# A hand-ordered kernel of two mixers: a new order of all its steps, and more partial sums left to TensorE

## The chip, the cores and the metric

One core of one Trainium2 chip runs one program. Its five engines (TensorE, VectorE, ScalarE, GpSimd and SyncE, in the profile PE, DVE, ACT, POOL and SP) each work through a list of instructions in a fixed order and wait for one another by semaphores. The metric is the device time of one execution in microseconds, lower being better.

## The reference

Two mixers run on the same input of 2048 positions and 512 channels, and a gate of each position blends them. All tensors are bfloat16.

```python
def reference(A_u, A_A_re, ..., B_x, B_wqkv, B_w_phi, B_wo, gate_w):
    ...
        K = jnp.einsum("dn,dnl,dn->dl", Cc, P, dB).real      # P = exp(dt * A * l): a kernel of 2048 taps per channel
        ...
        Yf = Uf * Kf[None, :, :, :]                          # long convolution by a Fourier transform over 4096 points
        ...
        phi_q = jnp.concatenate([_softmax(pq, axis=-1), _softmax(-pq, axis=-1)], axis=-1)
        phi_k = jnp.concatenate([_softmax(pk, axis=-1), _softmax(-pk, axis=-1)], axis=-1)
        kv = jnp.einsum("bhsf,bhsd->bhfd", phi_k, v)         # 32 heads of 16
        z  = jnp.einsum("bhsf->bhf", phi_k)
        num = jnp.einsum("bhqf,bhfd->bhqd", phi_q, kv)
        den = jnp.einsum("bhqf,bhf->bhq", phi_q, z)[..., None] + 1e-6
    ...
    x = A_u
    g = _sigmoid((x * gate_w).sum(-1, keepdims=True))
    a = _A_ref(x, ...)                                       # the state space model, as a convolution, plus u * Dskip
    b = _B_ref(x, B_wqkv, B_w_phi, B_wo)                     # the linear attention
    return g * a + (1 - g) * b
```

## The kernel before

The program is a list of some 870 **steps**. A step is a Python function that issues a handful of instructions on one engine; `Plan.add` records its name, its engine, the steps it needs, and the buffers it takes from and gives back to small rings (`take`, `drop`). Nothing schedules them by rule: `Plan.run` issues them in the order of one string, `ORDER`, in which two digits of base 64 are the number of a step. What an engine does next, and in which sequence its queue issues transfers, is therefore the order of its own steps in that string. Steps that may run on either of two engines (the copies out of PSUM, as `XK` or `oT`, on ACT or DVE) take their engine from the string `SIDES`; steps that may take a PSUM buffer from either of two rings take it from `RINGS`.

The work, in the order in which it begins:

- *Tables and input.* Sines and exponentials for the Fourier matrices (`W1`, `TB`, `TI`, `TJ`) and for the state space model (`Ctab`, `Dtab`, `Gtab`). The input `UD` is turned by TensorE (`xps`) and copied to `xT` (eight steps, each on DVE or ACT). `udc` copies `UD` into the layout `UDp` that the Fourier stages want (eight steps of a quarter of a half, DVE or ACT). `sel1` multiplies two small masks into `selE` (DVE or POOL).
- *Keys and input spectrum.* For 8 pairs of position blocks: `pk` (TensorE), its exponentials `ek` (ACT), the sums of 16 features `zk`, `vp`, `vb`, `vr`, and `kn`, which adds to `kvp`. A pair with a 1 in the string `ZPS` first lets TensorE add four by four (`zp`, 8 matmuls), so that DVE reduces one 128x512 tile to 128x128 (L739); a pair with a 0 has DVE reduce two 128x1024 tiles (L736). Between them `psAu`, `psBu` transform the input, and the result goes to memory (`xuw`). `kvbd` builds the block matrices of the attention from `kvp` after the last `kn`.
- *Units and queries.* The 512 channels are 16 **units** of 32. Unit U has DVE multiply the tables `Ctab` and `Dtab` twice (`A1`, `A2`, L1101), which makes two halves of the tile `A`. A unit with a 0 in the string `FOURS` then has DVE add the halves (`A3`, L1112) and TensorE multiply them with `R` (step `kps`, line 183) in 64 matmuls of 64 columns. A unit with a 1 leaves the addition out, and `kps` is 128 matmuls that add in PSUM. `R` comes from `cs` (two sines on ACT) and `E` (an exponential on ACT) by way of `El`, `Rh`, `Rl` on DVE. ACT needs another function table for sines than for exponentials, so the sines are done in four groups of four units, with a table load (L65) on either side. Behind `kps` stand `KD` (copy out), `psA`, `XA`, then per quarter of the channels `psB`, `XK`, the product `t` with the input's spectrum (DVE; its input `XUX` is loaded by `xup`), `psz`, `Zr`, a store `zw` and a load `zr` that turn the tile by way of memory into `ZT`, `psy`, and the gated result `ou` (DVE). Steps of the last unit work on half tiles. The queries (`pq`, `eq`, `zs`, `z1` to `z5`, a store `aw` and a load `ar` that spread the normalisers into `ax`, `em`, `ops`, `oT`) lie between them; the fourth query block is `pqL` and so on, and `bpsL` with `bsg` makes its output. `ax` and `ZT` share a single buffer, so each load of it waits for the last reader before it.
- *Output.* `out` and `outL` store from `xT`; each of the steps `out` may be issued from SP or from ACT.

```python
    def run(self):
        ...
        for n in self.nodes:
            n.at = n.eng if isinstance(n.eng, str) else n.eng[int(next(sides, 0))]
        ...
        for i in order:
            n = self.nodes[i]
            ...
            n.fn()
```

A 4-term unit is made by this line of `kgen_chunk`:

```python
            terms = [(k, k) for k in range(2)] if not four else [(0, 0), (2, 0), (1, 1), (3, 1)]
```

Of the kernel before, what the change touches and what calls it, by code (L numbers as in the profile page):

```python
# [70 lines left out]
class Plan:  # L71

    DIGITS = "0123456789abcdefghijklmnopqrstuvwxyzABCDEFGHIJKLMNOPQRSTUVWXYZ-_"
    ORDER = ("040B0H0K0d0y0C0D0L0s0I070J0M0P0g000S110j0N08010z0T0m0Q0e2R0a0p0q0r0_0W2T100U0O0V14120Y2U2x0A2S050k130Z2y2V2X2Z0R190v0t0u"
             "0b0c0w2_0l0E0X2W1516172L1a061b2Y022-30311y33340n030f0-"
             "0h1e1f0i1w2J18321c0F0o2B2K2M1n1z1H1g1A1o2D2C1d1p1I091x1E1J351Q1R2F1B0x1C2E0G2H1q36372G2I2P382N2Q391F3b2O3c4C1S3a4J4L4K4M"
             "3d3e4Q4R3f4U1Y3g4N1r4O1h4V3h1L4Y4-"
             "4P3i4Z4_3j4W4S53542z57504T3k4X1Z515b5d58521s1D593l5c3n5i5e55565j3m5a1G3o5q5f5g5s5r5t3p3r3q1T5m5n5u3s5v5h5o5k5w5x5B1P4D4E"
             "3w2v5l5p4F5y5F5C3y1U5H3x5G5I5J5z5A1V5D5E3t3z5U3D5K5V5M5N3A3R3E2w3F5W5L1O5_3G5O5Q5X5Y5Z3B3C1W605R5S1N3K3M1K3S1M5-"
             "5P3L634G642A615T653N673T6869626a666m6n6o3U6p3V3W3X3Y6b6c6q6d6r6s1t3Z3H3-1X3_3O1i1j41401_4221431-"  # L80
             "1k1l204445466e272923222b282d4748243P491m2a4a2c2e4b4g2f4c2g4d252h2o4e4h4i4n1u4j3u3v2j4p2i2l2k2m2q2p6i262s4q4o1v4k2n4u2r2t"
             "6f4v4w6j4r3I2u4x4y4z6g4l8l3J4A8p8m6t6u6k6v8q3Q4f4s6x6h8k8o6l8n8r8s6y6z6w6A6C4m4t4B8C6G8t6I6K8w8x8y8u6B6H6J4H8D8v6L6M6N7d"
             "8z8A8E4I8B7e7f8I7g8F6F9e8Q8G8H9b6O6P8R7h7j7i6Q6R8J9f7M7N8S6S6T6U6Vaeaf7O8W8X8K7k9g8L8T8U8Z8-"
             "938M8N7l6D8_7m8V7n6W6X6Y8O8P8Y7P94an7o7pao7q6_70717r90917Qa47S9295ag7R6Z7s6-"
             "72aha8a9966Ea7akaca5ai73aa75979998ajap7677a69aalatamab74ad7TaBaC7t797u7v7U78au7y7z7V7w7x9caq9naras7AavaH7W9d9h9o9paw7X9v"
             "aY9waK7Y7ZaDaL9q9raZ7a9x9y9zaIc57B7-aM9kc69D9EaQaEbX9L7Cb_aF7D9M7_9Ac07EaRaG9iaxaz80ay9B818285bYaA7Ga-"
             "7IaJ86879j9Fc19s7Jb-"
             "9l9m9Na_7bc7aNaOaPc3cbb2b37HbZc283aS9C7FaT849G9H9I9t89aUaWaV8baX7cccc8c99O9u9P9Q9R888cb87Kb9b0c4caceb19J8abacfcgbg8dck9K"
             "8ecl8f8gbbbh8hbcbibob4cP9Sbpbqcd9T8ichci7L8jcBcCcjcsdYcYctcucycDczdZd-cQcR9Ucmd_cHcvcw9W9Xcnbj9VbwbkblbxcocIbre0eLcp9Ze1"
             "e2b5b6eMbse3eUeVcxb7bye4cqbtbu9Ybdbe9-"  # L90
             "9_cAcrcSbme5cZdOdScEbfcFcGcTcUe6a0a1bve7dTdRdWeNa2e8cJcKe9bzbAedeecLeRcNcOa3eSeaebeOcMc_ePbBd0ecd1d7cVd8d9cWeCdfcXeWdPdU"
             "d2daefege-e_eQd3dbdQdgeTdVd4dndodXdhdcg1g2dieDeEdjeXbKfAbCbnbDbEbFeYfBeZf0f1bGc-dpbLddg7dqbHd5f2drbMf3f4f5bNfGbIbJbOezdk"
             "eAfDdsfEeBeIf6f7feffdldtbPdebQdBfCfHehdueifFejdmf8fgeJd6ekdvfIfJdyf9fafhfbg4fifKg5g6dwfjdzfkfcdxdCdEfLdAdFfMg3g8dGg9dHfN"
             "fleFelfdfmfpdDdLgagbgcgddIeGemeKfqeHfOfPfQfRgeenepfneofreqeresgfggghgifSfTfUfofsbRgjbSgkdJftetglfVfYfZgmgngobUbVgqfufWdM"
             "dNbWgpf-fvfxfygreufwevewexbTeydKfzfXf_g0gvgwgsgtgugx")
# [564 lines left out]
def attention_keys(P, nc, g, psum, r):  # L660
# [40 lines left out]
    for s2 in range(8):  # L701
# [20 lines left out]

        def ps4(K=K, box=box, on=P.ZPS[s2] == "1"):
            if not on:
                return
            box.ps = bank("zk")
            for u in range(2):
                e = K.E[:, u].rearrange("p g (h a b) -> p (g h) a b", a=4, b=4)
                for k in range(4):
                    nc.tensor.matmul(box.ps[:, 256 * u:256 * u + 256], lhsT=g.ident[:], rhs=e[:, :, k, :], start=(k == 0), stop=(k == 3), skip_group_check=True)  # L730

        def rd(K=K, box=box, on=P.ZPS[s2] == "1"):
            K.Z = g.kwk.tile([128, 2, 2, 32], F32, name="Zk")
            if not on:
                for u in range(2):
                    nc.vector.tensor_reduce(out=K.Z[:, u].rearrange("p g h -> p (g h)"), in_=K.E[:, u].rearrange("p g (h f) -> p (g h) f", f=16),  # L736
                                            axis=mybir.AxisListType.X, op=ALU.add)
                return
            nc.vector.tensor_reduce(out=K.Z[:].rearrange("p u g h -> p (u g h)"), in_=box.ps[:].rearrange("p (z b) -> p z b", b=4), axis=mybir.AxisListType.X, op=ALU.add)  # L739
# [888 lines left out]
```

## Time and profile before

| | us |
|---|---|
| three runs | 265.06, 265.24, 267.37 |
| median | 265.24 |
| profiled execution, first to last instruction (span) | 263.7 |
| median above that span | 1.5 |
| DVE, ACT, PE busy within the span | 233.9, 221.3, 198.5 |
| mean granted TensorE clock | 0.916 of full speed |

The profile is of one execution. Its span leaves out what lies before the first and after the last instruction, and no time of its own is listed for it beside the span; the three runs lie 1.4 to 3.7 us above it, the median 1.5 us. "Busy" is the time in which an engine has at least one instruction under way. Two DVE or ACT instructions behind one another overlap a little, so the second of two adds less than its own duration.

### The profile page before, as it was taken

Reading aid. Unit: us, or ns where it says so; the run is one execution under the profiler, and the core shown is the slowest. Engines: PE = TensorE matmul, PEld = TensorE weight load, DVE = VectorE, ACT = ScalarE, POOL = GpSimd, SP = SyncE. Lnnn points to the kernel's source line nnn. Section 1 sums busy time; section 2 is a strip of 40 time slices with the busy share of each in tenths; the row PEclk is TensorE's granted clock in tenths of the full one; section 3 lists DMA queues with packets and bytes.
Section 4 is the critical chain, followed back from the end, with each engine's and each line's share of the span. In section 5 each row is a group of like instructions: output and inputs, shape, how many; then the busy total and the mean of one; then the engine's idle time right before and its main releaser. Section 6 shows DMA issues by size and latency. Waiting matters only on the chain.

```text
span 263.7 us, 10050 instructions
## 1 busy us (share of the span) xinstructions
PE 198.5 (75%) x4491; PEld 133.8 (51%) x4512; DVE 233.9 (89%) x315; ACT 221.3 (84%) x305; POOL 8.3 (3%) x21
## 2 busy tenths in 40 slices
PE   0755999999845688988565867889996678979770
PEld 0654656646634423446354245665674456764550
DVE  6799989888799989999999999999999999986630
ACT  6989999998899989998999899999998996744200
POOL 4700000000000000000000000000000000000000
PEclk9999999999995659997999579999999999998975
DMA  6899000454500885203343366239753599989576
GB/s 196 144 204 233 6 4 2 121 146 138 151 10 2 239 239 165 83 13 87 88 162 82 122 209 210 73 116 199 150 193 120 189 239 242 179 206 141 133 112 102
DMA packets 67547, 35.93 MB, mean 136 GB/s; under 512 B 46000, under 2 KB 62000, under 8 KB 67504
## 3 DMA queue, kind: packets, MB, share of 16 engines
q1 hardware_dynamic: 65648, 34.76, 55.0%
q10 hardware_dynamic: 1856, 0.52, 1.1%
q8 instruction: 35, 0.57, 1.0%
q14 instruction: 8, 0.07, 0.1%
HBM read 22.17 MB, written 13.11 MB: 134 GB/s over the span
## 4 chain that ended last, share of the span: by engine, by line
PE 32%; DVE 26%; ACT 13%; DMA 12%; issue 7%; SPq 7%; DVEq 0%; ACTq 0%
PE pk L709 5%; DMA ax<-apd 5%; PE vp L757 5%; DVE A L1101 3%; SPq L1494 3%; DMA ZT<-Zd 3%; DMA apd<-apm 3%; ACT cs L68 3%; DVE R L1123 2%; DVE R L1119 2%; PE psz L1265 2%; PE psA L591 2%; PE bps L946 2%; PE psB L616 2%; PE kvp L774 2%
## 5 line engine op out<-in xcount | busy, mean ns | idle before, releaser
L1101 DVE TENSOR_TENSOR A<-Ctab,Dtab 128x2048 bf16<-128x2048 bf16 x32 | 37.9, 1220 | 0.0
L68 ACT ACTIVATE cs<-args 128x1024 bf16<-128x1024 f32 x32 | 30.8, 1042 | 1.5 <-PE args L1023 1.5
L1265 PE MATMUL psz<-t,TI 128*128 128x512 bf16 x51 | 16.5, 414 | 6.2 <-DVE t L1233 4.6
L1123 DVE TENSOR_TENSOR R<-E,cs 128x2048 bf16<-128x2048 bf16 x16 | 19.5, 1219 | 0.1
L1119 DVE TENSOR_TENSOR R<-E,cs 128x2048 bf16<-128x2048 bf16 x16 | 19.5, 1219 | 0.0
L68 ACT ACTIVATE Ek<-pk 128x512 bf16<-128x512 f32 x32 | 16.7, 600 | 1.9 <-PE pk L709 1.6
L183 PE MATMUL kps<-R,A 128*32 128x64 bf16 x1536 | 17.2, 203 | 1.5 <-DVE A L1112 0.4
L183 PEld LDWEIGHTS <-A 128*32 128x32 bf16 x1536 | 15.3, 117 | 5.6 <-issue 2.0
L149 ACT CAST Zr<-psz 128x1024 bf16<-128x1024 f32 x15 | 15.5, 1032 | 3.2 <-PE psz L1265 1.5
L149 ACT CAST XA<-psA 128x1024 bf16<-128x1024 f32 (+1 forms) x15 | 14.7, 1017 | 3.4 <-PE psA L190 3.4
L757 PE MATMUL vp<-WW,xT 128*128 128x512 bf16 x59 | 16.9, 419 | 0.5 <-issue 0.3
L616 PE MATMUL psB<-XAu,TB 64*128 64x128 bf16 x256 | 11.8, 250 | 6.6 <-ACT xst L149 3.5
L1233 DVE TENSOR_TENSOR t<-XUX,XK 128x2048 bf16<-128x2048 bf16 x14 | 16.7, 1219 | 0.0
L68 ACT ACTIVATE E<-args 128x1024 bf16<-128x1024 f32 x16 | 16.4, 1036 | 0.3 <-PE args L1045 0.2
L68 ACT ACTIVATE Eq<-pq 128x512 bf16<-128x512 f32 (+1 forms) x28 | 16.5, 694 | 0.1
L149 ACT CAST XK<-psB 128x1024 bf16<-128x1024 f32 (+1 forms) x14 | 13.7, 993 | 2.8 <-PE psB L196 1.5
L843 PE MATMUL pq<-xT,Wqp 128*128 128x512 bf16 x64 | 15.4, 379 | 0.8 <-ACT xT L149 0.6
L709 PE MATMUL pk<-WW,xT 128*128 128x512 bf16 x58 | 15.0, 380 | 0.4 <-issue 0.2
L190 PE MATMUL psA<-W,KD 128*64 128x128 bf16 x256 | 10.7, 233 | 5.5 <-ACT KD L149 2.7
L616 PEld LDWEIGHTS <-TB 64*128 64x128 bf16 x256 | 9.7, 111 | 9.9 <-issue 9.8
L196 PE MATMUL psB<-XA,TB 128*128 128x128 bf16 (+2 forms) x192 | 10.6, 206 | 3.6 <-DVE XA L151 1.6
L190 PEld LDWEIGHTS <-KD 128*64 128x64 bf16 x256 | 8.5, 117 | 9.1 <-issue 5.2
(210 smaller groups left out, 502.0 us busy)
## 6 DMA issues: line engine op xcount, KB each, us to landing
XUX<-XUd SPq DMA_DIRECT2D x32, 256.0 KB
XUd<-xst SPq DMA_DIRECT2D x8, 512.0 KB
ax<-apd SPq DMA_DIRECT2D x16, 256.0 KB
Zd<-Zr SPq DMA_DIRECT2D x15, 256.0 KB
ZT<-Zd SPq DMA_DIRECT2D x6, 512.0 KB
UD<-in_A_u_dram SPq DMA_DIRECT2D x16, 128.0 KB
XUd<-xst SPq DMA_DIRECT2D x8, 256.0 KB
wqk<-in_B_wqkv_dram SPq DMA_DIRECT2D x1, 1024.0 KB
```

Of the source, the lines that this page charges most:

```text
L68: return self.nc.scalar.activation(**kw)
L149: self.nc.scalar.copy(out=o, in_=i)
L183: nc.tensor.matmul(kps[32 * dj:32 * dj + 32, g4, e, :], lhsT=A[:, d // 4, 32 * ka:32 * ka + 32, d % 4], rhs=R[:, kr, d, :], start=(i == 0) ...
L190: nc.tensor.matmul(ps[64 * ri:64 * ri + 64], lhsT=lhsT, rhs=fc.W1[:, ri].rearrange("p r d -> p (r d)"), start=True, stop=True, tile_positi ...
L616: nc.tensor.matmul(box.ps[:, c2, sl, :], lhsT=fc.TB[rows, b0:b0 + 2].rearrange("p a b -> p (a b)"), rhs=X.t[rows, k, r0 + sl].rearrange("p ...
L709: nc.tensor.matmul(box.ps[:], lhsT=xT[:, st, kt, :], rhs=g.WW[:, kt, :], start=(kt == 0), stop=(kt == 3))
L757: nc.tensor.matmul(box.ps[:], lhsT=xT[:, st, kt, :], rhs=g.WW[:, 4 + kt, :], start=(kt == 0), stop=(kt == 3))
L1101: nc.vector.tensor_tensor(out=c.A[:, :, 64 * k:64 * k + 64, :].rearrange("p q (x b) l -> p x b q l", b=8), in0=cf.unsqueeze(2).to_broadcas ...
L1119: nc.vector.tensor_tensor(out=c.R[:, :, :, 32:64], in0=t.E[:, 1].unsqueeze(1).to_broadcast([128, 2, 32, 32]), in1=t.cs[:], op=ALU.mult)
L1123: nc.vector.tensor_tensor(out=c.R[:, :, :, 0:32], in0=t.E[:, 0].unsqueeze(1).to_broadcast([128, 2, 32, 32]), in1=t.cs[:, ::-1, :, ::-1], o ...
L1233: nc.vector.tensor_tensor(out=box.t, in0=Ls[r0 // ns].X[:], in1=box.XK[:].unsqueeze(1).to_broadcast([128, 2, 1024]), op=ALU.mult)
L1265: nc.tensor.matmul(box.ps[:, hb, :], lhsT=fc.TI[:, k].rearrange("p t h a -> p (t h a)"), rhs=box.t[:, k, 512 * hb:512 * hb + 512], start=( ...
```

## The change

All of it is in the strings at the head of `Plan`. `ORDER` is another permutation of the same steps, made with steps that are dense in TensorE work put apart. `SIDES` and `RINGS` are other choices. `FOURS` has ones for units 0 to 14 (before: 1, 2, 3, 4, 7, 9, 11 and 12), so that units 0, 5, 6, 8, 10, 13 and 14 lose their `A3` on DVE and get 64 more matmuls each. `ZPS` has ones for the pairs 5, 6 and 7 (before also 1), so that pair 1 loses its 8 matmuls `zp` and gets two reductions in place of one. The other change of engine counts, by steps: `oT` three more on DVE and three fewer on ACT; `udc` three more on DVE; `xT` one more on DVE; `XK` two fewer on DVE; `sel1` from DVE to POOL; one `bs3` to ACT and one `bsg` to DVE; among the `out` steps, one from ACT to SP and one from SP to ACT.

```diff
 class Plan:
     ...
-    ORDER = ("040B0H0K0d0y0C0D0L0s0I070J0M0P0g000S110j0N08010z0T0m0Q0e2R0a0p0q0r0_0W2T100U0O0V14120Y2U2x0A2S050k130Z2y2V2X2Z0R190v0t0u"
...
+    ORDER = ("1d0405060B0C0D0d0e0f0y0z0A0s0t0u0H0I0J0M0L000708090g0h0i0j0k0l0P0Q0K0102030S0U0V0N2R2T0_2x0O0T0W0Y0m0n0o0a0b0c0X10111415"
...
-    FOURS = ("0111100101011000")
-    ZPS = ("01000111")
+    FOURS = ("1111111111111110")
+    ZPS = ("00000111")
```

What this does to the engines' lists shows at three places. Line numbers of the changed kernel are 4 smaller from line 100 on.

The first place is VectorE's list ahead of the keys, where the last `xT` tiles and the `udc` copies stand. Before:

```order
L383 TENSOR_TENSOR ppy<-psri,ppx 128x512
L151 COPY xT<-xps 128x1024 x2
L151 COPY UDp<-UD 128x2x8x64
L383 TENSOR_TENSOR ppx<-psri,ppx 128x512
L151 COPY xT<-xps 128x1024
L151 CAST XAu<-psA 128x256x4 x2
```

With the change:

```order
L379 TENSOR_TENSOR ppy<-psri,ppx 128x512
L147 COPY UDp<-UD 128x2x8x64
L379 TENSOR_TENSOR ppx<-psri,ppx 128x512
L147 COPY xT<-xps 128x1024
L147 COPY UDp<-UD 128x2x8x64 x2
L147 COPY xT<-xps 128x1024
L147 COPY UDp<-UD 128x2x8x64
L147 COPY xT<-xps 128x1024
L147 CAST XAu<-psA 128x256x4 x3
```

Three copies to `UDp` have come over from ScalarE and stand ahead of VectorE's last `xT`, of which it now has five in all.

The second place is VectorE's list for the units 14 and 15, up to the last instruction that the last `kps` needs. The row `A<-A` is the addition `A3`, `A<-Ctab` is `A1` or `A2`, `E<-E` is `El`, `R<-E` is `Rh` (the smaller line number) or `Rl`. Before:

```order
L1119 TENSOR_TENSOR R<-E,cs 128x64x32
L1101 TENSOR_TENSOR A<-Ctab_75,Dtab 128x64x8x4 x2
L1365 TENSOR_TENSOR xT<-psy,gT 128x4x128
L1053 TENSOR_TENSOR E<-E,Gtab 128x1024
L1123 TENSOR_TENSOR R<-E,cs 128x64x32
L1112 TENSOR_TENSOR A<-A 128x8x256
L1233 TENSOR_TENSOR t<-XUX,XK 128x2048 x2
L1101 TENSOR_TENSOR A<-Ctab_75,Dtab 128x64x8x4 x2
L1112 TENSOR_TENSOR A<-A 128x8x256
L1053 TENSOR_TENSOR E<-E,Gtab 128x1024
L1123 TENSOR_TENSOR R<-E,cs 128x64x32
```

With the change:

```order
L1115 TENSOR_TENSOR R<-E,cs 128x64x32
L1049 TENSOR_TENSOR E<-E,Gtab 128x1024
L1119 TENSOR_TENSOR R<-E,cs 128x64x32
L1361 TENSOR_TENSOR xT<-psy,gT 128x4x128
L1115 TENSOR_TENSOR R<-E,cs 128x64x32
L1097 TENSOR_TENSOR A<-Ctab_75,Dtab 128x64x8x4
L1229 TENSOR_TENSOR t<-XUX,XK 128x2048 x2
L1097 TENSOR_TENSOR A<-Ctab_75,Dtab 128x64x8x4
L1049 TENSOR_TENSOR E<-E,Gtab 128x1024
L1119 TENSOR_TENSOR R<-E,cs 128x64x32
L1097 TENSOR_TENSOR A<-Ctab_75,Dtab 128x64x8x4
L1108 TENSOR_TENSOR A<-A 128x8x256
```

The addition of unit 14 is gone, that of unit 15 stands last, and `Rh` of unit 15 has moved behind `Rl` of unit 14.

The third place is the end of SyncE's list: the stores `Zd<-Zr` (`zw`), the loads `ZT<-Zd` (`zr`), the stores of the result from L1382 (`out`) and L995 (`outL`). Before:

```order
L1188 DMA XUX<-XUd 128x1024 x2
L1287 DMA ZT<-Zd_0_122 64x32x64 x2
L1382 DMA out_dram<-xT 32x12x128 x4
L1278 DMA Zd_64_123<-Zr 128x1024
L1382 DMA out_dram<-xT 32x12x256 x2
L995 DMA out_dram<-xT 32x4x384 x2
L1287 DMA ZT<-Zd_64_123 64x32x32 x2
L1382 DMA out_dram<-xT 512x1x64 x4
L995 DMA out_dram<-xT 32x4x384 x2
L1382 DMA out_dram<-xT 512x1x64 x2
```

With the change:

```order
L1184 DMA XUX<-XUd 128x1024 x2
L1378 DMA out_dram<-xT 32x12x256 x2
L1283 DMA ZT<-Zd_0_122 64x32x64 x2
L1378 DMA out_dram<-xT 32x12x128 x2
L1274 DMA Zd_64_123<-Zr 128x1024
L1378 DMA out_dram<-xT 32x12x128 x2
L1378 DMA out_dram<-xT 32x12x256 x2
L1283 DMA ZT<-Zd_64_123 64x32x32 x2
L1378 DMA out_dram<-xT 512x1x64 x2
L991 DMA out_dram<-xT 32x4x384 x4
L1378 DMA out_dram<-xT 512x1x64 x2
```

Behind the last `ZT` load two of the four stores of 512 short rows are gone (ScalarE issues them now, ahead of its last copy out of PSUM), and two stores of long rows have come in their place; both stores of 256 columns now stand ahead of that load.

More of the change, by code (lines that the diff above doesn't have):

```diff
@@ L73 @@
     DIGITS = "0123456789abcdefghijklmnopqrstuvwxyzABCDEFGHIJKLMNOPQRSTUVWXYZ-_"
-    ORDER = ("040B0H0K0d0y0C0D0L0s0I070J0M0P0g000S110j0N08010z0T0m0Q0e2R0a0p0q0r0_0W2T100U0O0V14120Y2U2x0A2S050k130Z2y2V2X2Z0R190v0t0u"
[L75 to L95, printed above, removed]
@@ L100 @@
+    SIDES = ("111110011110111001000000111010001001001100001011100000000000010100001101111101000010100111000000000000000000000000000000"
+             "00000001000000010000000110010000000001000000010001001")
+    RINGS = ("101000001110111011100000000000000000000000100000000000000010111111100000001011100011010110001101000101101100111010011101"
+             "01000")
     WARM = ("000000000000000000000000000000000000000000000000000000000000000000000000000000000000000000000000000000000000000000000000"
```

21 lines of the change are left out of this document (17 added, 4 removed).

## The prediction

> **What bounds the kernel now.** I read the page's first part, then cut the span into six stages by what the engines wait for in the chain that ended last, and asked for the busy time of each engine in each.
>
> ```profile
> PE 198.5 (75%) x4491; PEld 133.8 (51%) x4512; DVE 233.9 (89%) x315; ACT 221.3 (84%) x305; POOL 8.3 (3%) x21
> ...
> 0.00:28.00 28.00, 13.89 (x160) 12.32 (x161) 23.54 (x56) 24.90 (x32) 8.33 (x21) 1.00 0.94 184
> 28.00:71.00 43.00, 42.42 (x749) 26.22 (x757) 37.60 (x52) 39.02 (x75) 0.00 (x0) 1.00 0.30 84
> 71.00:104.50 33.50, 22.15 (x312) 12.90 (x313) 32.34 (x55) 31.50 (x36) 0.00 (x0) 0.75 0.46 132
> 104.50:214.20 109.70, 84.28 (x2219) 55.44 (x2225) 107.81 (x117) 104.93 (x138) 0.00 (x0) 0.94 0.48 134
> 214.20:235.60 21.40, 18.77 (x472) 15.03 (x473) 20.86 (x20) 15.66 (x17) 0.00 (x0) 1.00 1.08 211
> 235.60:263.70 28.10, 17.03 (x585) 11.91 (x585) 11.79 (x17) 5.34 (x10) 0.00 (x0) 0.76 0.73 124
> ```
>
> The columns behind the length are busy time of PE, weight loads, DVE, ACT and POOL, then the granted TensorE clock. The 89% of DVE hide three regimes. From 28 to 71 us (keys and input spectrum) PE is busy 42.42 of 43.00 us: that stage is TensorE's. From 71 to 235.6 us DVE works 161.0 of 164.6 us, but up to 214.2 us ACT is hardly behind it (104.93 of 109.70): two engines share that bound. After 235.6 us both are mostly idle, and a chain of single steps sets the end. So DVE work is worth its time only in the middle, and only as far as ACT can follow.
>
> **The change part by part.** The prices:
>
> ```profile
> L1112 DVE TENSOR_TENSOR A<-A 128x2048 bf16<-128x2048 bf16 x8 | 9.8, 1221 | 0.1
> L736 DVE TENSOR_REDUCE Zk<-Ek 128x64 f32<-128x1024 bf16 x8 | 9.3, 1210 | 0.0
> L739 DVE TENSOR_REDUCE Zk<-zk 128x128 f32<-128x512 f32 x4 | 2.8, 692 | 1.4 <-PE zk L730 1.3
> L730 PE MATMUL zk<-Ek,ident 128*128 128x256 bf16 x32 | 4.2, 277 | 0.0
> ...
> 25.16 1.28 DVE L151 COPY xT<-xps 128x1024 bf16<-128x1024 bf16 x2
> 26.35 0.42 DVE L151 COPY UDp<-UD 128x1024 bf16<-128x1024 bf16 x1
> 28.02 1.89 PE L709 MATMUL pk<-WW,xT 128*128 128x512 bf16 x7
> ...
> 135.19 0.68 DVE L151 CAST wo<-ops 128x512 bf16<-128x512 f32 x1
> 135.79 1.22 DVE L1123 TENSOR_TENSOR R<-E,cs 128x2048 bf16<-128x2048 bf16 x1
> ...
> 209.69 1.26 PE L183 MATMUL kps<-R,A 128*32 128x64 bf16 x128
> 217.16 0.73 PE L183 MATMUL kps<-R,A 128*32 128x64 bf16 x64
> 227.81 1.93 ACT L149 CAST oT<-ops 128x1024 bf16<-128x1024 f32 x2 [1.16 <-PE ops L932]
> 229.62 0.60 ACT L149 CAST KD<-kps 128x512 bf16<-128x512 f32 x1
> 230.09 2.35 DVE L1101 TENSOR_TENSOR A<-Ctab,Dtab 128x2048 bf16<-128x2048 bf16 x2
> ```
>
> A DVE instruction of 2048 elements lasts 1.22 us, but two in a row take 2.35, so one more costs 1.13 in a full queue; a copy of 512 columns lasts 0.68 and the next starts 0.60 later.
>
> *To the first `pk` (28 us).* VectorE gets three `udc` (0.42 each, 1.26) and one `xT` (two take 1.28, so 0.64 or less, by the pitch 0.60) ahead of its last `xT`, which every `pk` needs: 1.9 by durations, about 1.7 with the overlap. DVE and ACT are both full here from 8 us on, and the pieces that ACT loses are filled by exponentials that it had done later, so nothing hides this: **+1.7**. `sel1` moves to POOL, and what POOL does beside VectorE shows here:
>
> ```profile
> 4.06 0.81 DVE L269 TENSOR_SCALAR tgv<-tgc,if,one 128x1024 int32<-128x1024 f32 x1
> 8.16 1.06 POOL L473 TENSOR_TENSOR Wphi<-wc,mask 128x512 bf16<-128x512 bf16 x1 [4.34 <-DMA wc<-in_B_w_phi_dram]
> 8.30 1.46 DVE L269 TENSOR_SCALAR tgv<-tgc,one 128x1024 int32<-128x1024 f32 x1 [2.18 <-ACT TB L68]
> ```
>
> The same DVE form takes 0.81 us alone and 1.46 beside a POOL product. `sel1` is a product of twice the elements (an estimate from the 1.06 us row: 2.1 us on POOL). It costs DVE between 0 (if tensor-by-tensor products stand beside it) and 2 x 0.65 = 1.3; I take **+0.3**, near the lower end, since most of what follows on DVE there waits for copies anyway.
>
> *Keys (28 to 71 us).* TensorE loses eight `zp` matmuls (4.2 / 32 x 8 = 1.05). VectorE gains two reductions of 1.21 for one of 0.69 and loses `sel1`; it has 43.00 - 37.60 = 5.4 us idle in the stage, which hides that. **-1.0**. If the reductions delayed the exponential of pair 1 and with it a `kn`, up to 1.7 would come back.
>
> *71 to 104.5 us.* Both engines are nearly full, and ACT's list is the same set. VectorE loses `A3` of unit 0 but does `kvbd` ahead of `A1`, so it waits for the last `kn` with nothing behind it to do. **0**, with 1 either way.
>
> *104.5 us to the last `kps`.* Three lower bounds stand side by side, and the latest decides.
> - VectorE: 7 additions less, 7 x 1.13 = 7.9, and three `oT` more, 3 x 0.60 = 1.8: -6.1.
> - ScalarE: between the first table load and the last its list loses three `oT` of 512 columns (0.60 each) and gains an `oT` of 1024 (0.97): -0.8, if its 4.8 us of waits in this stage stay. After the last load the new order has `E`, two `Zr`, `KD`, two `XA` and then the `E` of unit 15: 7 x 0.91 = 6.4 us (0.91 is 1.93 less 1.02, the second of two). Then VectorE has `Rh`, two products, two `t`, `A1`, `El`, `Rl`, `A2`, `A3`: with the two products being `A2` of unit 14 and `A1` of unit 15, that is eight of 1.13 and one of 0.60, 9.6. With the load itself (1.28) 17.3 us, where it was 21.4 before (214.2 to 235.6). Together -0.8 - 4.1 = -4.9.
> - The chain over `ax` and `ZT`, whose rows are:
>
> ```profile
> 210.97 4.62 SPq L1287 DMA_DIRECT2D ZT<-Zd  x2
> 219.00 0.63 PE L1343 MATMUL psy<-ZT,TJ 64*32 64x128 bf16 x32 [1.11 <-DMA ZT<-Zd]
> 226.74 1.91 PE L932 MATMUL ops<-Eq,KVbd 128*128 128x256 bf16 x16
> 234.34 1.22 DVE L1123 TENSOR_TENSOR R<-E,cs 128x2048 bf16<-128x2048 bf16 x1
> 235.62 0.51 PE L1343 MATMUL psy<-ZT,TJ 64*32 64x128 bf16 x22 [1.43 <-issue]
> 237.00 1.05 PE L183 MATMUL kps<-R,A 128*32 128x64 bf16 x64
> ```
>
> The load of `ZT` leaves when the last `em` has given `ax` back, lands 8 us later, and from 219.00 to 237.00 TensorE has no pause but the 1.43. Up to that `em` VectorE has five additions less and three `oT` more (-5.7 + 1.8 = -3.9). Then the same 8 us, and the same 18 us of TensorE: two units cost 1.26 instead of 0.73 (+1.1), a `psz` comes behind the load (+1.0), both `ops` go (-1.9). So -3.7 with the 1.43 in it.
>
> I take the latest, **-3.7**; the range runs from -6.1 to -0.9 (ACT's own saving alone, if its waits grow by what VectorE gives). `kps` of unit 15 then starts at 237.0 + 1.7 + 0.3 - 1.0 - 3.7 = 234.3.
>
> *Tail, 26.7 us from 237.0 on.*
>
> ```profile
> 249.25 3.14 PE L1299 MATMUL psz<-TI,t 128*32 128x64 bf16 x128 [1.88 <-DVE t L1236]
> 251.63 6.97 SPq L1382 DMA_DIRECT2D out_dram<-xT  x4
> 256.59 0.69 DVE L1368 TENSOR_TENSOR xT<-psy,gT 128x512 bf16<-128x512 f32 x1 [0.51 <-PE psy L1343]
> 259.84 1.26 SPq L1382 DMA_DIRECT2D out_dram<-xT  x2
> ```
>
> One `ops` step comes behind the last `kps`, ahead of everything that TensorE does for the end: 1.91 / 2 = +1.0 (1.9 at half clock). The copies `XK` go from two engines to ACT alone and no longer wait for a `bsg` on DVE: -0.6, the duration of one. The last VectorE step ends at 257.28, but its store is issued at 259.84: SyncE is still busy with four stores of short rows (6.97). In the new order two of the four are ACT's, and two stores of long rows take their place. 257.28 is the earliest it can be, so at most -2.56; ACT's two stores stand ahead of its last copy `Zn`, which may give some back. I take **-2.0**. Tail: -1.6.
>
> **Sum.** +1.7 + 0.3 - 1.0 + 0 - 3.7 - 1.6 = -4.3. The profiled span of 263.7 becomes 259.4; the median lies 1.54 above the span, so 260.9 against 265.24.
>
> **The clock.** The added 448 matmuls, less 8, change where TensorE pauses.
>
> ```profile
> 117.00:120.00 3.00, 0.82 (x31) 0.50 (x18) 3.00 (x4) 3.00 (x5) 0.00 (x0) 1.00 0.12 27
> 120.00:123.00 3.00, 3.00 (x78) 2.45 (x72) 2.71 (x3) 2.24 (x4) 0.00 (x0) 0.57 0.23 67
> 129.00:132.00 3.00, 1.02 (x60) 0.62 (x46) 2.87 (x3) 3.00 (x4) 0.00 (x0) 1.00 0.06 13
> 132.00:135.00 3.00, 1.83 (x26) 1.30 (x25) 3.00 (x4) 3.00 (x4) 0.00 (x0) 1.00 0.34 102
> ```
>
> Three microseconds with 0.82 of TensorE work are followed by 0.57 of the clock; three with 1.02, spread out, by the full clock. In the last `kps` the clock is already down (1.05 us for the 64 matmuls that took 0.73). [...]
>
> **The rivals.**
> 1. *As summed*: 260.9, between 258 and 263.5. For it: three independent bounds within 2.4 us of one another. Chance 0.55.
> 2. *VectorE's list alone decides*: ACT uses its 4.8 us of waits to follow, and the transfer behind the last `em` lands sooner. Then -6.1 and the full -2.6 + 0.4 at the end: 265.24 + 1.0 - 6.1 - 2.2 = 257.9. For it: ACT's waits here are mostly for results of VectorE. Against: 8 us for `ZT` is a transfer, which VectorE cannot shorten. Chance 0.2.
> 3. *The relief turns into waits on ACT* (the change does not do what it says): per unit both engines have about the same work once the addition is gone, so VectorE stops at `Rh` and `t` for `E`, `cs` and `XK`; -0.9, and the `ops` in the tail eats the gain of the stores: 265.24 + 1.0 - 0.9 = 265.3. Chance 0.15.
> 4. *Slower: TensorE cold in the last two stages.* From 219 to 247 us TensorE is the pacing engine. A cold stretch of 10 us there (0.75 of the clock on average in the row 71.00:104.50 is 8.4 us of lost clock) costs 5 us; two cost 10, and with the gains of this sum that is 260.9 + 10 = 270.9. It decides from 7 us of lost clock time on. For it: the two added sums of units 13 and 14 lie there, and `kps` of unit 15 has to wait for VectorE, a pause ahead of the tail. Against: the row 214.20:235.60 shows 1.00. Chance 0.1.
>
> **Chances and range.** A difference of 1% (2.65 us) is about what a measurement of this kernel can tell from no change. Faster by more than that means below 262.6: nearly nine tenths of case 1 (0.48) and case 2 (0.2), 0.68. Within 1%: the rest of case 1 and case 3, 0.22. Slower: 0.10. The range goes from 256.0 (case 2 and a tail at full clock) to 265.5 (case 3); it leaves out case 4 and some ends of the others.
>
> **What would show it.** In the changed profile: `A<-A` x1 and `kps` x1984 in the groups; DVE busy about 6 us less between the first `A1` and the last; the first `pk` near 30 us (wrong if at 28: then VectorE had room there); PE still full up to the last `zp`; waits of DVE for `E`, `cs` or `XK` of some 2 us in the middle, where there were almost none; the last `kps` near 234; the last store issued within half a microsecond of the last `ou`. The prediction is wrong if the TensorE clock is down for long between 214 us and the end, if a load of `ax` makes `em` wait, or if ScalarE's `Zn` stands behind its stores.

## The result: 3% slower

The changed kernel took 274.24 us (median of four runs, 273.05 to 277.15) against 266.31 us of the kernel before (four runs beside it). The ratio is 1.031 with a 95% interval of 1.023 to 1.039. Forecast were 260.9 us, at most 265.5. The profiled execution has a span of 271.0 us where it was 263.7.

### The profile after

The first part of the page, then the six stages again, cut near the same steps (first `pk`, last sums of the keys, first units, last table load, 1.5 us ahead of the last `kps`):

```profile
PE 200.4 (74%) x4932; PEld 138.0 (51%) x4952; DVE 230.1 (85%) x313; ACT 217.8 (80%) x300; POOL 10.0 (4%) x22
...
0.00:32.20 32.20, 16.02 (x160) 14.33 (x161) 26.93 (x61) 24.74 (x33) 9.99 (x22) 0.84 0.83 168
32.20:74.50 42.30, 41.72 (x743) 25.39 (x750) 37.97 (x52) 35.71 (x69) 0.00 (x0) 1.00 0.26 75
74.50:109.50 35.00, 23.04 (x339) 13.68 (x339) 34.10 (x60) 34.81 (x41) 0.00 (x0) 0.85 0.49 142
109.50:220.80 111.30, 86.12 (x2547) 59.50 (x2551) 103.30 (x112) 102.83 (x133) 0.00 (x0) 0.92 0.51 136
220.80:241.50 20.70, 16.94 (x547) 13.28 (x549) 17.83 (x17) 12.15 (x14) 0.00 (x0) 1.00 0.84 182
241.50:271.00 29.50, 16.56 (x607) 11.79 (x605) 9.95 (x15) 7.55 (x13) 0.00 (x0) 0.82 0.65 119
```

VectorE lost work in the two stages of the units, the fourth and the fifth, about as forecast: 121.1 us there instead of 128.7. But the long fourth stage has not become shorter: 111.3 us, before 109.7. (The last table load starts at 218.94 us, 1.9 us ahead of the cut; up to it the stage is 109.4 us, where it was 109.7.) Both engines that had set its pace wait there now: VectorE is idle for 8.0 us of it, where it was 1.9, and ScalarE for 8.5, where it was 4.8. What they wait for stands in the groups of instructions: the idle time ahead of a group, and what ended it, is behind the second bar.

```profile
L1097 DVE TENSOR_TENSOR A<-Ctab,Dtab 128x2048 bf16<-128x2048 bf16 x32 | 38.5, 1221 | 6.0 <-PE kps L179 5.9
L179 PE MATMUL kps<-R,A 128*32 128x64 bf16 x1984 | 22.2, 205 | 9.0 <-issue 4.6 <-DVE R L1119 1.6 <-DVE A L1097 1.5
```

`A1` waits 5.9 us for `kps`, because there is a single tile `A` and the next unit's products may overwrite it only when `kps` has read it; before, it never waited. And `kps` itself stands still for 4.6 us with "issue": TensorE waits for nothing that the profile shows. The timeline has nine pauses of half a microsecond or more of this kind; the bracket gives the idle time ahead of the row:

```profile
122.15 0.24 PE L863 MATMUL zs<-Eq,SSw 128*32 128x128 bf16 x3 [0.57 <-issue]
131.25 0.78 PE L179 MATMUL kps<-R,A 128*32 128x64 bf16 x43 [1.16 <-issue]
145.23 0.22 PE L863 MATMUL zs<-Eq,SSw 128*32 128x128 bf16 x1 [1.01 <-issue]
201.02 0.22 PE L179 MATMUL kps<-R,A 128*32 128x64 bf16 x3 [1.87 <-issue]
221.01 0.22 PE L822 MATMUL psy<-diagD,xT 128*128 128x128 bf16 x1 [0.58 <-issue]
229.38 0.39 PE L1339 MATMUL psy<-ZT,TJ 64*32 64x128 bf16 x13 [0.50 <-issue]
239.86 0.35 PE L1339 MATMUL psy<-ZT,TJ 64*32 64x128 bf16 x12 [1.63 <-issue]
244.96 0.52 PE L179 MATMUL kps<-R,A 128*32 128x64 bf16 x37 [1.56 <-issue]
261.16 0.66 PE L1352 MATMUL psy<-Z,TJ 64*32 64x16 bf16 x63 [1.28 <-issue]
```

They make 10.2 us. The kernel before had two at such places, 1.43 us at 235.62 (a row that the prediction shows) and 0.23 near the end; beside these, either profile has a few gaps of 0.16 to 0.33 us without a releaser elsewhere, which are not counted here. Counting from the start shows what they have in common. Here are the windows from 0 to the end of three of the pauses; the second number in brackets is the count of weight loads so far:

```profile
0.00:131.20 131.20, 96.56 (x1868) 63.29 (x1880) 120.54 (x198) 116.41 (x178) 9.99 (x22) 0.92 0.45 114
0.00:201.00 201.00, 151.94 (x3528) 102.86 (x3544) 184.54 (x265) 180.70 (x255) 9.99 (x22) 0.92 0.48 125
0.00:244.90 244.90, 185.73 (x4420) 127.83 (x4439) 221.94 (x301) 211.84 (x289) 9.99 (x22) 0.92 0.54 135
```

1880 and 3544 are 1664 apart, 13 times 128; all nine counts leave 87 or 88 when divided by 128, and so does the 3927 of the pause at 235.62 before. Every matmul here comes with one weight load (4932 and 4952 on the page), so 128 of them are 256 instructions: TensorE's program seems to arrive in blocks of 256, and a pause looks like the wait for the next block. The page's part on DMA queues fits: it lists a queue of 16 KB transfers,

```profile
q8 instruction: 38, 0.62, 1.1%
```

38 of them for the 9884 instructions of TensorE (260 each), 35 before. Each of the nine pauses ends 2.4 to 3.3 us after the start of such a transfer.

Where the time went, by the starts of the same steps:

| us | before | after | this stage forecast | measured |
|---|---|---|---|---|
| first `pk` | 28.0 | 32.2 | +2.0 | +4.2 |
| last exponentials of the keys | 67.1 | 70.6 | -1.0 | -0.7 |
| first `A1` | 99.8 | 104.8 | 0 | +1.5 |
| last `kps` starts | 237.0 | 243.0 | -3.7 | +1.0 |
| last `ou` ends | 257.3 | 266.6 | +0.4 | +3.3 |
| end | 263.7 | 271.0 | -2.0 | -2.0 |

### The profile page after: what moved, and what is told of

Its sections match the earlier page's. It is cut to its first block, busy times and chain, and to the rows that moved or that the text cites. A ratio compares the mean times of both kernels' runs of the same rounds, so it can differ in the third digit from the quotient of the medians.

```text
span 271.0 us, 10929 instructions
## 1 busy us (share of the span) xinstructions
PE 200.4 (74%) x4932; PEld 138.0 (51%) x4952; DVE 230.1 (85%) x313; ACT 217.8 (80%) x300; POOL 10.0 (4%) x22
## 4 chain that ended last, share of the span: by engine, by line
PE 40%; ACT 23%; DVE 19%; issue 11%; DMA 6%; SPq 0%; DVEq 0%; ACTq 0%
PE kps L179 5%; PE pk L705 5%; PE vp L753 5%; PE psy L820 3%; PE psz L1261 3%; ACT XA L145 2%; ACT Eq L68 2%; DVE A L1097 2%; DMA ax<-apd 2%; DVE R L1115 2%; ACT xst L145 2%; ACT E L68 2%; ACT Zr L145 2%; ACT trg L68 2%; PE kvp L770 2%
## 5 line engine op out<-in xcount | busy, mean ns | idle before, releaser
L1097 DVE TENSOR_TENSOR A<-Ctab,Dtab 128x2048 bf16<-128x2048 bf16 x32 | 38.5, 1221 | 6.0 <-PE kps L179 5.9
L179 PE MATMUL kps<-R,A 128*32 128x64 bf16 x1984 | 22.2, 205 | 9.0 <-issue 4.6
L179 PEld LDWEIGHTS <-A 128*32 128x32 bf16 x1984 | 20.2, 118 | 12.9 <-issue 7.4
L145 ACT CAST XK<-psB 128x1024 bf16<-128x1024 f32 (+1 forms) x16 | 15.2, 982 | 5.1 <-PE psB L192 5.0
L1261 PE MATMUL psz<-t,TI 128*128 128x512 bf16 x52 | 15.2, 393 | 2.8 <-ACT KD L145 1.1
L753 PE MATMUL vp<-WW,xT 128*128 128x512 bf16 x59 | 15.7, 386 | 0.5 <-issue 0.3
L145 ACT CAST KD<-kps 128x1024 bf16<-128x1024 f32 (+2 forms) x10 | 8.5, 863 | 5.8 <-PE kps L179 5.8
L186 PE MATMUL psA<-W,KD 128*64 128x128 bf16 x256 | 10.1, 230 | 3.0 <-ACT cs L68 1.6
```

Of the source, the lines that this page charges most:

```text
L145: self.nc.scalar.copy(out=o, in_=i)
L179: nc.tensor.matmul(kps[32 * dj:32 * dj + 32, g4, e, :], lhsT=A[:, d // 4, 32 * ka:32 * ka + 32, d % 4], rhs=R[:, kr, d, :], start=(i == 0) ...
L753: nc.tensor.matmul(box.ps[:], lhsT=xT[:, st, kt, :], rhs=g.WW[:, 4 + kt, :], start=(kt == 0), stop=(kt == 3))
L1097: nc.vector.tensor_tensor(out=c.A[:, :, 64 * k:64 * k + 64, :].rearrange("p q (x b) l -> p x b q l", b=8), in0=cf.unsqueeze(2).to_broadcas ...
L1261: nc.tensor.matmul(box.ps[:, hb, :], lhsT=fc.TI[:, k].rearrange("p t h a -> p (t h a)"), rhs=box.t[:, k, 512 * hb:512 * hb + 512], start=( ...
```

## Experiments

Theory 1: the added four-term sums cost time by their instructions, because TensorE's supply of them has become a limit. Rivals: the new order costs it; the added matmuls cost it by their own time on TensorE; GpSimd's product at the start does; a buffer or a transfer stops TensorE at certain steps. "Pauses" below is the sum of the unexplained pauses at the border of a block. All ratios are to the kernel before, run beside each.

| run | order, units with sums | ratio (95%) | pauses, us |
|---|---|---|---|
| before | old, 8 | 1 | 1.7 |
| after | new, 15 | 1.031 (1.023-1.039) | 10.2 |
| e1_new_order_old_sums | new, 8 | 0.999 (0.996-1.002) | 1.7 |
| e2_old_order_new_sums | old, 15 | 1.036 (1.030-1.041) | 14.0 |
| e3_shift_128 | new, 15 | 1.027 (1.022-1.032) | 11.0 |
| e4_old_head | new with old start, 15 | 1.034 (1.028-1.041) | (14.1) |
| e5_loads_ahead | new, 8 | 1.012 (1.005-1.018) | 2.7 |
| e6_old_head_old_sums | new with old start, 8 | 1.015 (1.010-1.021) | 3.7 |
| e7_old_head_old_sums_loads | new with old start, 8 | 1.015 (1.007-1.022) | 2.4 |
| e9_tiny_for_sums | new, 8 and 448 tiny matmuls | 1.052 (1.046-1.058) | (5.1) |
| e10_sel1_back | new, 15 | 1.027 (1.022-1.032) | 12.4 |
| e11_old_sums_sel1 | new, 8 | 0.990 (0.986-0.993) | 3.5 |
| e12_true_old_head | new with old start, 8 | 0.989 (0.985-0.993) | 3.6 |
| e13_before_sel1_pool | old, 8 | 1.000 (0.996-1.003) | 2.9 |
| e14_no_sums | new, 0 | 1.024 (1.016-1.033) | 1.9 |
| e15_four_sums | new, 4 | 1.025 (1.017-1.033) | 5.9 |
| e16_twelve_sums | new, 12 | 1.017 (1.010-1.024) | 9.0 |
| e17_shift_best | new, 8 | 1.041 (1.033-1.049) | 7.1 |

The two numbers in brackets come from profiles with a granted clock of 0.88 and 0.78 and are not compared with the others. The kernels with 15 units have the long pauses and the long times, but the pauses are not all of it: those of e5, e6 and e7 are much like those of e11 and e12, and the times are 2 to 3% longer. What is known of that stands below; the rest is open.

### The sums or the order

```diff
 # e1: the changed kernel
-    FOURS = ("1111111111111110")
+    FOURS = ("0111100101011000")
 # e2: the kernel before
-    FOURS = ("0111100101011000")
+    FOURS = ("1111111111111110")
```

> The changed kernel with the FOURS of before: units 0, 5, 6, 8, 10, 13 and 14 get their addition on VectorE back (7 x 1.13 = 7.9 us of VectorE) and lose 64 matmuls each (896 of TensorE's 9904 instructions, 3.5 blocks of 256). Theory 1, TensorE's instructions are fetched in blocks of 256 and the fetch takes longer than a dense block runs: the pauses of TensorE that nothing in the profile explains (10.2 us in nine places in the changed kernel) fall to about half, VectorE's waits for kps (5.9 us) fall below 2 us, and the time is 1 to 4 us below that of the changed kernel. Theory 2, the new order alone costs the time and the sums help as predicted: 4 to 6 us above the changed kernel.

> The kernel before with the FOURS of the change and nothing else: 7 additions less on VectorE, 448 matmuls (896 instructions) more on TensorE, every step in its old place. Theory 1 (fetch of blocks of 256 instructions): pauses without a releaser rise from 1.7 us to 5 us or more, VectorE waits for kps because the single tile A is held longer, and the time is within 2 us of before or above it. Theory 2 (the sums help, the order costs): 3 to 5 us below before.

Measured 0.999 and 1.036. In either order the seven added sums cost 3.2 to 3.6%, 8.4 to 9.5 us, and the pauses rise by 8.4 and 12.3 us. With the old start (e4 and e6 below) it is 1.9%, with `sel1` on VectorE (e10 and e11) 3.8%. Theory 2 is out: all the rest of the change together (order, engines, PSUM rings, `ZPS`) comes to nothing in sum. VectorE gave up 7.9 us of additions in both and the time did not fall. The loss is larger than the 1 to 4 us that were expected from Theory 1, and in e1 VectorE no longer waits for `kps` at all. The added matmuls by their own time are less than half of it: `kps` keeps TensorE busy for 22.2 us in the changed kernel and 18.5 in e1, 3.7 less.

### Does a pause belong to the work or to the count

```diff
         box.ps = psum([128, 4, 512], "wtp", BF16)
+        for _ in range(64 if h == 0 and first else 0):
+            nc.tensor.transpose(out=box.ps[:, 0, 0:16], in_=g.ident[0:16, :], identity=g.ident[0:16, 0:16])
```

> The changed kernel with 64 tiny transposes (128 instructions, half a block of 256) ahead of TensorE's first step, where it waits 7 us for its weights anyway. Theory 1 (fetch): every unexplained pause moves by half a block. Counted in weight loads from the start, the pauses stay at 87 or 88 modulo 128; in the work they move: in kps of unit 3 from ahead of matmul 86 to ahead of matmul 22, in kps of unit 11 from ahead of matmul 126 to ahead of matmul 62, and out of the middle of kps of unit 15. The time may go either way by 2 us. Rival (a buffer, PSUM or a transfer stops TensorE at these steps): the pauses stay at the same matmuls of the same steps.

Three of its eight pauses, and the counts up to them:

```profile
196.70 0.26 PE L179 MATMUL kps<-R,A 128*32 128x64 bf16 x7 [1.47 <-issue]
227.58 0.34 PE L822 MATMUL psy<-wo,oT 128*128 128x128 bf16 x3 [1.98 <-issue]
240.24 0.38 PE L179 MATMUL kps<-R,A 128*32 128x64 bf16 x21 [4.38 <-issue]
...
0.00:196.65 196.65, 152.38 (x3400) 101.98 (x3416) 180.30 (x261) 176.65 (x251) 9.97 (x22) 0.90 0.47 123
0.00:227.53 227.53, 174.20 (x4037) 117.08 (x4055) 207.86 (x287) 201.80 (x277) 9.97 (x22) 0.92 0.51 131
0.00:240.19 240.19, 181.19 (x4293) 123.41 (x4311) 214.77 (x293) 206.96 (x283) 9.97 (x22) 0.92 0.52 132
```

3416, 4055 and 4311 again leave 88 or 87, with 64 loads of other work ahead: the pauses stay with the count and move in the work, so no buffer of a certain step is their cause. The pauses have left the places in units 3, 11 and 15, but at the two new places that were named, in units 3 and 11, the border passes without one: a border is where a pause can be, not where it must be. Their sum and the time stayed about the same (11.0 us, 1.027).

### Instructions without the sums

```diff
 def kgen_chunk(nc, kps, A, R, four, pad=None):
+    for _ in range(0 if pad is None else 64):
+        nc.tensor.matmul(kps[0:32, 0, 0, 0:16], lhsT=pad[0:16, 0:32], rhs=pad[0:16, 0:16], start=True, stop=True, skip_group_check=True)
```

> The new order with the old FOURS, and in kps of units 0, 5, 6, 8, 10, 13 and 14 64 tiny matmuls (16 rows, 16 columns, overwritten at once) ahead of the 64 real ones. TensorE gets the instruction count of the changed kernel (896 more), at less work than the added matmuls, and VectorE keeps its additions. Theory 1 (instruction fetch): unexplained pauses of 8 us or more in all, again at 87 or 88 modulo 128 weight loads, and 5 us or more above the same kernel without them, which equals before. Rival, the added sums cost by their work on TensorE or by the tables' sum itself: less than 3 us above before, pauses of 2 us or less.

Ratio 1.052 (1.046 to 1.058), 5.3% above e1. But the tiny matmuls were not short. The trace has them at each of the seven units as in this one, with the 64 real matmuls behind them:

```profile
117.79 1.75 PE L174 MATMUL kps<-ident 16*32 16x16 bf16 x64
119.48 0.73 PE L181 MATMUL kps<-R,A 128*32 128x64 bf16 x64
```

With a thirty-second of the multiplications they take 1.75 us for 64, where 64 real ones take 0.73 and 64 added ones 0.53 (1.26 less 0.73). Over seven units that is 12.3 us of TensorE, about as much as the whole loss of 14 us. And the pauses at the borders, in this profile with a clock of 0.78, make 5.1 us, not the 8 or more that were expected. So this run does not separate the number of instructions from the time that they hold TensorE, and it is no evidence for Theory 1.

### The start

```diff
 # e4, e6, e7: all steps up to the second pk in order, engines and PSUM buffers of before; e4 with 15 units of sums, e6 and e7 with 8
 # e7 and e5: ZT loads of the last quarter ahead of four stores
-zw.14 out.2 out.1 zr.8 zr.9 out.5 ...
+zw.14 zr.8 zr.9 out.2 out.1 out.5 ...
```

> All steps up to the second pk in the order, on the engines and in the PSUM buffers of before; everything behind it as in the changed kernel. In the traces the first pk came at 32.20 us instead of 28.02. If the start is a cost that nothing later absorbs: 4 us below the changed kernel. If the stages behind it absorb it (a transfer or an engine that is late anyway): within 1.5 us of the changed kernel.

> The new order with the old FOURS (equal to before within 0.3%), and the steps up to the second pk as in before. The start then costs 4 us less. With TensorE's fetch no longer the limit behind it, 2 to 4 us should reach the end: ratio to before 0.985 to 0.993. If something behind absorbs the start (as it did with the new sums), 0.999.

> The kernel of the old head and the old sums in the new order, and the two last ZT loads ahead of the four stores. If the loads' place costs 2 us or more in the new order whatever stands ahead: 2 us less than without it, ratio to before 0.977 to 0.987. If the loads end up waiting for the same stores in another way: no difference.

1.034 (1.028 to 1.041), 1.015 (1.010 to 1.021) and 1.015 (1.007 to 1.022): no gain from the old start in any, and with the old sums (e6) a loss of 1.6% against e1. It was not truly the old start: `sel1` comes behind the second `pk` in the old order, so it had stayed on GpSimd, which does it as soon as it is free. What that does is seen in the changed kernel:

```profile
10.32 3.43 DVE L265 TENSOR_SCALAR tgv<-tgc,one 128x1024 int32<-128x1024 f32 x1
10.41 1.90 POOL L454 TENSOR_TENSOR selE<-m,b 128x1024 bf16<-128x1024 bf16 x1
```

A VectorE operation that takes 0.81 us alone (7.22 us, the same form) lasts 3.43 beside GpSimd's product and the `KVbd` fill behind it (12.25 us, 0.95 long), 2.6 more. Four kernels put that one step elsewhere:

```diff
 # the engine of one step, a digit of SIDES
-sel1  POOL
+sel1  DVE
```

> The changed kernel with one step on its old engine: sel1 on VectorE again, where it stands in the middle of the keys (1.22 us there, in idle time). In the changed kernel a VectorE operation of 0.81 us lasted 3.43 us while GpSimd made that product (10.41 to 12.31 us), 2.6 us more. Theory A, GpSimd's product stops VectorE and the delay reaches the end: the operation lasts 0.8 us, the first pk comes about 2.6 us earlier, the time is 2 to 3 us below the changed kernel (ratio to before about 1.021). Theory B, the added sums alone set the end: no change (1.031).

> The new order with the old FOURS and sel1 on VectorE. Without the added sums it equalled before (0.999). Theory A (GpSimd's product costs 2 to 3 us at the start, and nothing absorbs it): ratio to before 0.988 to 0.992, faster than both kernels. Theory B (absorbed): 0.999.

> As the kernel with the old head and the old sums (1.015), but with sel1 on VectorE, so that the start is truly that of before: there sel1 had run on GpSimd at 10.8 us, and a VectorE operation of 0.20 us lasted 2.85 us beside it. Theory A: first pk at 28 us, 2.5 us or more below that kernel, ratio to before 1.005 or less. If what follows the start in the new order cannot use an earlier start: 1.010 to 1.015.

> The kernel before with a single step moved: sel1 on GpSimd, all else as it was. Theory A: a VectorE operation at about 11 us is stretched by 2 to 3 us, the first pk comes at 30 to 31 us, the time is 2 to 3 us above before (ratio 1.008 to 1.011). Theory B, the loss at the start is absorbed by the stages that TensorE or ScalarE sets: 1.000 to 1.003.

With the old sums it is worth 0.9% (e11, 0.990 against 0.999), and e11 is faster than both kernels: 264.84 us, where the kernel before took 266.89 beside it. With the new sums it is not separable (e10, 1.027 against 1.031), and the reason shows in the first and last start of two lines, of the changed kernel and then of e10:

```profile
L705 PE MATMUL pk<-WW,xT x58: 379/379/390, 32.2 to 71.0; 128*128 128x512 bf16 x58
L179 PE MATMUL kps<-R,A x1984: 189/198/242, 113.8 to 245.3; 128*32 128x64 bf16 x199
...
L705 PE MATMUL pk<-WW,xT x64: 379/379/390, 29.0 to 67.8; 128*128 128x512 bf16 x64
L179 PE MATMUL kps<-R,A x1984: 189/198/243, 110.5 to 245.3; 128*32 128x64 bf16 x199
```

The first `pk` and the first `kps` come 3.2 and 3.3 us earlier, the last `kps` at the same 245.3: the pauses on the way, up to the start of the last `kps`, grew from 7.3 to 10.4 us and took it. e12 (0.989, 0.985 to 0.993) with the true old start equals e11, so with the old sums the copies `udc` and `xT` on VectorE cost nothing that reaches the end. But e12 is also e6 with nothing changed but the engine of `sel1`, and there that one step is worth 2.6%, some 7 us, more than the 2.65 us by which it stretched VectorE; why is open. And e13, the kernel before with `sel1` on GpSimd, is not slower at all (1.000, 0.996 to 1.003):

```profile
11.39 1.95 POOL L454 TENSOR_TENSOR selE<-m,b 128x1024 bf16<-128x1024 bf16 x1
...
11.51 1.21 DVE L147 CAST WW<-wps 128x1024 bf16<-128x1024 f32 x1
12.64 1.25 DVE L265 TENSOR_SCALAR tgv<-tgc,one 128x1024 int32<-128x1024 f32 x1
```

There a copy out of PSUM ran beside the product and lasted its usual 1.21 us; only the end of it touched a `tgv`, which lasted 1.25 us. The first `pk` came at 29.1 us instead of 28.0, and the end does not show it. What GpSimd's product cost in these two runs differs with what VectorE did just then: 2.6 us on a `tgv` beside it and the fill, 0.44 on one beside its end, nothing on the copy. The cause was not tested. My expectation of 2 to 3 us for e13 was wrong.

### The end of SyncE's list

> The changed kernel with one exchange at the end of SyncE's list: the two loads ZT<-Zd of the last quarter stand ahead of the four stores of the steps out.2 and out.1 instead of behind them. In the changed kernel the second of these loads waits 5.0 us for a store and the last psy waits 2.7 us for the load. If that store's place is the cause: the second load is issued within 1 us of the first, and the time is 2 to 3 us below the changed kernel (3.1% above before becomes about 2.2%). If the end is late for TensorE's instruction fetch alone: within 1 us of the changed kernel.

By a slip this kernel also had the old FOURS, so its base is e1 and not the changed kernel. It measured 1.012 (1.005 to 1.018), slower than e1. SyncE's last rows in e1, then here:

```profile
249.56 5.51 SPq L1283 DMA_DIRECT2D ZT<-Zd  x2
255.51 1.64 SPq L1378 DMA_DIRECT2D out_dram<-xT  x2
257.26 3.63 SPq L991 DMA_DIRECT2D out_dram<-xT  x4
260.99 1.27 SPq L1378 DMA_DIRECT2D out_dram<-xT  x2
...
250.30 2.34 SPq L1283 DMA_DIRECT2D ZT<-Zd  x2
252.69 6.97 SPq L1378 DMA_DIRECT2D out_dram<-xT  x6
259.77 4.28 SPq L991 DMA_DIRECT2D out_dram<-xT  x4
264.14 1.25 SPq L1378 DMA_DIRECT2D out_dram<-xT  x2
```

The second load no longer waits (both within 2.34 us), but the last `ou` starts at 259.2 instead of 258.9 all the same: the pause ahead of the last `psy`, 1.7 us instead of 1.3, took most of the 0.7 us that `psy` had waited for the load, and the last `kps` had started 0.5 us later. The stores that were pushed back then end 3.1 us later. The wait was worth little beside that pause, and its removal was paid for in the queue.

### How many sums

```diff
 # the kernel of e11
-    FOURS = ("0111100101011000")
+    FOURS = ("0000000000000000")   e14
+    FOURS = ("0010100001001000")   e15
+    FOURS = ("1111101111011010")   e16
```

> The new order with sel1 on VectorE (0.990 of before with 8 units of four-term sums) and FOURS zero for every unit: 8 additions more on VectorE (8 x 1.13 = 9.0 us), 1024 instructions less on TensorE. If TensorE's instruction supply limits only above 8 units, VectorE decides here: 7 to 9 us more, ratio 1.016 to 1.024, no unexplained pause over 0.5 us but the last. If the supply already limits with 8 units: below 1.005.

> The same with four-term sums in units 2, 4, 9 and 12 alone: 4 additions more than with 8 units (4.5 us), 512 instructions less. VectorE decides: 1.003 to 1.007. Supply already limits with 8: 0.985 to 0.990.

> The same with the 8 units and 0, 6, 8 and 14 as well: 4 additions less (4.5 us of VectorE), 512 instructions more. Supply theory: the pauses grow by about 4 us and eat what VectorE saves, ratio 1.000 to 1.015. By the prediction's pricing (0.5 us of TensorE for 1.13 us of VectorE): 0.975 to 0.985.

> The new order with 8 units of sums and sel1 on VectorE (0.990), and 64 tiny transposes (half a block of TensorE's instructions) ahead of TensorE's first step. In that kernel three pauses of 0.7, 1.0 and 1.7 us stood at weight loads 1751, 3671 and 4439 (87 modulo 128), the last of them 6 us ahead of the end. All move by 64 loads of work. If the place of the last pause matters: 1 to 2 us less or more (0.983 to 0.987, or 0.994 to 0.997). If not: 0.990.

With none the eight additions cost 3.4%, 9.1 us for 9.0 us of work on VectorE, as expected. With twelve the four additions saved (4.5 us) are outweighed: pauses 5.5 us longer, 2.7% slower than e11, about what Theory 1 expected and far from the prediction's pricing. Four should have been between none and eight and is as slow as none (expected 1.003 to 1.007): one pause of 3.49 us stands in it. Of the counts tried eight was the fastest, but no ranking follows, and e17 says why. It is e11 with 64 tiny transposes ahead, at a time when TensorE waits for its weights, with no other work added. At most 0.7% either way was expected, and it is 5.2% slower. In its profile the first product of unit 8 still starts as early as in e11 (163.4 and 163.7 us); all that is lost comes behind it. The largest of its pauses, with the row of TensorE that ends it and then the stretches around it (busy time of PE, weight loads, VectorE, ScalarE, GpSimd; clock, share of the DMA engines):

```profile
187.47 0.23 PE L865 MATMUL zs<-Eq,SSw 128*32 128x128 bf16 x1 [3.85 <-issue]
...
180.00:182.00 2.00, 2.00 (x127) 1.61 (x129) 2.00 (x4) 2.00 (x3) 0.00 (x0) 1.00 1.35 165
182.00:184.00 2.00, 1.45 (x73) 1.02 (x58) 2.00 (x3) 2.00 (x3) 0.00 (x0) 1.00 1.23 196
184.00:185.00 1.00, 0.00 (x0) 0.00 (x0) 1.00 (x2) 0.55 (x1) 0.00 (x0) 1.00 0.80 246
185.00:187.40 2.40, 0.00 (x0) 0.00 (x0) 0.43 (x1) 0.00 (x0) 0.00 (x0) 1.00 0.03 7
```

Nearly the whole core stands still. TensorE raced through one `kps` (128 matmuls in 1.26 us at 181.0) while the DMA engines were full (1.35, 1.23); the instruction queue's only transfer between 180 and 187 us started at 184.9, when they were draining, and 2.6 us later TensorE went on. As these traces read, the loss depends on three things at once: how quickly a block is used up, what the DMA engines carry then, and where the border falls. That the traffic delays the fetch is read from the traces; no run took the traffic away. Nor are e17's pauses, 3.6 us more than e11's, by their own length all of its 5.2%. VectorE's waits in the units stage rose from 2.2 to 11.0 us, about the 9.6 us by which the profiled span is longer. The longest, 3.4 us, stands right behind the pause of 3.85 us, and the next, 2.3 us for `kps`, behind the one of 1.44; the others were not followed.

## Why the prediction was wrong

The step that failed is the sum from 104.5 us to the last `kps`. It took the latest of three bounds, VectorE, ScalarE and the chain over `ax`, and priced an added sum on TensorE by its duration (1.26 us instead of 0.73). TensorE with its unexplained pauses was a fourth bound that the sum put at nothing, and with 896 more instructions, three and a half blocks, it came out later than the three: -3.7 forecast, +1.0 measured, with the pauses in that stretch at 7.3 us where one of 1.4 had been. In e1, the new order with the old sums, the same stretch is 1.9 us shorter than before, so the added sums lengthened it by 2.9 us instead of shortening it. How much of this is the wait for instructions and how much the 3.7 us of the added matmuls themselves no run separates. The clue was in the prediction's own rows: the 1.43 us "issue" at 235.62 was carried along as part of a chain and not asked about.

- *Start*: +2.0 forecast, +4.2 measured. `sel1` was taken at +0.3, with a bound of 1.3 from a shorter product; with the fill behind it, it stretched VectorE by 2.6 us. (That a product of two tensors beside it would lose nothing, the lower bound there, no run shows; beside it stood the `tgv` of 3.43 us.) In e10 the first `pk` comes 3.2 us earlier by this step alone, so only 1.0 of the 4.2 us is left for the copies, which were put at 1.7. And e12 shows that with the old sums their share does not reach the end, so "nothing hides this" was wrong as well.
- *Keys*: -1.0 forecast, -0.7 measured; right.
- *71 to 104.5 us*: 0 with 1 either way, +1.5 measured. VectorE and ScalarE are the fuller of work there, 34.10 and 34.81 us of 35.00 where it was 32.34 and 31.50 of 33.50; and ScalarE has 41 instructions there, not 36, so its list was not "the same set".
- *Tail*: the -2.0 for the last store is right to a tenth (6.4 us from the last `ou` to the end, now 4.4). What lies ahead was not: a pause of 1.56 us within the last `kps` and a wait of 2.7 us for `ZT`, whose load stood behind stores. The chain that ended last has both; from it the last pauses of TensorE, then its last steps:

```profile
238.23 1.63 issue
...
243.40 1.56 issue
...
256.26 4.71 DMA out_dram<-xT
260.99 4.36 DMA ZT<-Zd
265.89 0.69 DVE xT L1364
```

The pause of 1.28 us at 261.16 is not on it: the last `psy` waited for `ZT` longer. In e1, with the old sums, it is 24.9 us from the last `kps` to the end, as against 28.0 here and 25.1 forecast. So the tail's sum holds without the added sums and fails with them.

- *Rivals*: the slower case (0.1) was a cold TensorE, its clock down, in the last two stages; their clock is 1.00 and 0.82, where it was 1.00 and 0.76, so the sign came out by another mechanism. That a cold stretch of 10 us costs 5 us takes half the clock; the profile before has that value where the last `kps` lasts 1.05 us:

  ```profile
  237.00:238.00 1.00, 1.00 (x68) 0.91 (x66) 0.89 (x1) 0.48 (x1) 0.00 (x0) 0.50 0.07 16
  ```

  How much idle time brings the clock down is not shown: in e17 it stays at 1.00 through the pause of 3.85 us. The third rival had the right shape, relief turned into waits, but on the wrong engine: VectorE waits mostly for `kps` on TensorE (5.9 us). The 1.8 us for `XK` and 0.3 for `E` in the middle are the sign that the prediction had named, about 2 us; but 1.2 of it stands behind an `XK` that itself waited 1.0 us for TensorE's `psB`.
- *Order*: whether placing dense TensorE steps apart helps is not shown: with 15 units of sums the pauses are 10.2 us, where the old order has 14.0, but the times (1.031 and 1.036) cannot be told apart. With 8 units there was little to gain (1.7 us in both orders).

## What to carry to other kernels

Count TensorE's instructions as a resource of their own: here 448 more short matmuls came with 3.7 us more of `kps` and 8.4 us more of unexplained pauses (e1 against the changed kernel), so the price of one was not its duration alone, and pauses a multiple of 128 weight loads apart (each matmul has one load) were the sign. A dummy of little arithmetic need not be a short one (64 tiny matmuls took 1.75 us in e9, 64 real ones 0.73): look at its row before building an argument on it. Before moving work from VectorE to TensorE, ask which engine will be late next, and whether its instructions can arrive that fast. And compare variants of such a kernel with the borders in mind: half a block of idle instructions at the start moved the time of the same work by 5.2% in one kernel (e17 against e11) and by nothing that can be told in another (e3, 1.027 against 1.031).
